# A transformer block on one core: where the first norm of two chunks is scaled and transposed, under a new written-out order

## The chip, the cores and the metric

The kernel runs on one NeuronCore of a Trainium2 chip. The core has a matrix engine (TensorE, called PE; PEld is its weight load), a vector engine (VectorE, DVE), an activation engine (ScalarE, ACT), a general engine (GpSimd, POOL) and an engine that here only issues transfers (SyncE, SP). Each takes its own instructions strictly in order and waits on semaphores for the others. Transfers (DMA) are issued from the queues of SP, ACT or POOL and run beside all engines. The metric is device time in microseconds (us) for one execution. Before the change it is 195.86 us, the median of 3 runs (195.64 to 196.87).

## The reference

The input x has 2048 rows of 512 bf16 numbers. The block is an attention and a gated MLP, each behind a layer norm without weights:

```python
def _layernorm(x, axis=-1, eps=1e-5):
    m = jnp.mean(x, axis=axis, keepdims=True)
    v = jnp.var(x, axis=axis, keepdims=True)
    return (x - m) / jnp.sqrt(v + eps)
...
    h = x + _A_ref(_layernorm(x, axis=-1), A_wqkv, A_wo)
    h2 = h + _B_ref(_layernorm(h, axis=-1), B_W_gate, B_W_up, B_W_down)
```

`_A_ref` is attention with 32 heads of 16, in which a position sees only itself and 7 earlier positions in steps of 2 (`W, dil = 8, 2`), softmax over these 8, then `@ wo`. `_B_ref` is `(relu(x @ W_gate) * (x @ W_up)) @ W_down` with 1376 hidden columns.

## The kernel before

The 2048 rows are worked in four chunks of 512 rows, numbered 0 to 3; a chunk is four row blocks of 128. For each chunk the kernel goes through these stages. The names in brackets are the keys that the code gives its steps, and the prediction uses them with the chunk's number behind a dot.

- First norm: DVE takes the statistics of each row block (`xst`, L467, and `xag`, L470); ACT forms 1/sqrt(variance + eps) by Ln and Exp (`xrl`, L480, `xre`, L484); then x is scaled (`xxn`). The scaling has two forms in `f_xn`: on DVE by a tensor_scalar (L502), or on ACT by an activation with a scale and a bias per row (L499), for which DVE first makes the bias (`xnb`, L488). `LNA[0]` says by chunk which form is taken: before the change, ACT for chunks 1 and 3 and DVE for chunks 0 and 2.
- Transposition of the scaled rows: either PE transposes each row block by four 128x128 matmuls (`xtp`, L531) into a PSUM bank that ACT copies out, two row blocks at a time (`xte`, L547), or a DMA transpose issued by SP does it (`xtd`, L520). `DMAT` names the pairs of row blocks that go by DMA; before, these are both pairs of chunk 3's first norm and five pairs of the second norm.
- q, k and v: 12 groups of four 128x512 matmuls (`qkv0` to `qkv11`, L572), each copied out of its bank by ACT (`qe`, L580).
- Scores: DVE multiplies q by shifted views of k (`pr0`, `pr1`, L635 for chunk 0, L620 else), PE sums over the heads' columns with a selection matrix (`sc0`, `sc1`, L626), ACT takes the exponential (`ex`, L684), PE and ACT form the reciprocal of the softmax sum (`den`, `dl`, `dr`).
- Spreads: 8 DMAs per chunk on SP's queue copy the weights of each head over its 16 columns (`bd0S`, `bd1S`, L744).
- Product with v: DVE multiplies (`mu`, L791 for chunk 0, L776 else); for chunks 0 to 2 an accumulating DMA issued by POOL adds one half of the result to the other (`ta`, L819); DVE adds up the rest (`tree`, L779) and for chunk 0 scales (`om`, L783).
- Output projection on PE (`wo`, L855, L858), residual and row sums (`rs`), second norm (`hnm`, `hsq`, `hxn`, `htp`), and the MLP: gate and up products (`mm`, L928 and L895), ACT copies and Relu, DVE product (`gu`, L956), down product (`dn`, L978), last addition and the stores (`os`).

The late weights, the up and the down matrix, are loaded by four steps on SP's queue (`ldu`, `ldd`). They wait for a step of POOL that reads a result of chunk 0 (`lg`, L837 and L838).

The order of the work is not found while the kernel runs. Each step gets a rank by its number of creation from the table `RANK`, and every engine carries out its own steps in the order of their ranks. A planner places them with assumed durations; its times only decide which of several equal buffers a step gets: 8 PSUM banks are shared by all matmul outputs, 5 large buffers by products and spreads, 5 row buffers by scaled rows.

Of the kernel before, what the change touches and what calls it, by code (L numbers as in the profile page):

```python
# [17 lines left out]
RANK = [  # L18
# [38 lines left out]
]  # L57


# [143 lines left out]
def kernel(  # L203
# [171 lines left out]
    NHALF = 6  # L375
    XT = (3.5, 3.65, 5.6, 6.1, 8.5, 8.9, 9.4, 9.9, 15.9, 17.4)
    WT = (7.55, 7.55, 5.0, 14.2, 18.7, 25.5, 22.0, 29.0)
    DMAT = (('h',2,0),('h',2,2),('h',3,0),('h',3,2),('h',1,0),('x',3,0),('x',3,2))

    EARLY = (1, 2, 3)  # L380

# [12 lines left out]
    TTM, DTG, ATE = 0.0845, 0.35, 0.3  # L394
    LASTC = (D // 2, 3 * D // 4)

    LNA = ((0, 1, 0, 1), (0, 0, 0, 0))


    MM, TP = 0.2165, 0.057  # L400
# [32 lines left out]
    def layernorm(tk, src, dst_slots, pr, groups, on_act, residual=None):  # L433
# [7 lines left out]
        for grp in groups:  # L441
# [72 lines left out]
            for j0 in range(lo, hi, step):  # L514
                if (ln, tk, j0) in DMAT:
                    for j in range(j0, min(j0 + step, hi)):
# [38 lines left out]
    for tk in range(NCK):  # L555
# [3 lines left out]
        groups = XG[tk]  # L559
        xnT, xev = layernorm(tk, xload[tk], xnT_s, lnp, groups, LNA[0][tk])  # L560

# [314 lines left out]

        hnT, hev = layernorm(tk, hd, hnT_s, base + 52, HG[tk], LNA[1][tk], residual=sm)

# [186 lines left out]
```

## Time and profile before

| | before |
|---|---|
| median of 3 runs | 195.86 us (195.64 to 196.87) |
| the profiled execution | 197.74 us |
| its span, first to last instruction | 195.7 us |
| mean granted TensorE clock | 0.998 |
| busy: PE, DVE, ACT, POOL | 187.2, 148.6, 116.7, 18.9 us |
| instructions | 3063 |

The span is what the profile shows of one execution on the core; the execution's own time is 2.0 us longer. This execution was 1.9 us slower than the median of the runs, so a difference that is worked out from its rows is set against 197.74 us and then carried over to the median. In rows of a timeline the first number is the start in us from the span's beginning and the second how long the group of instructions lasted; what stands in brackets is the idle time of the engine before them and what ended it. A row of a group gives busy time, mean ns of one and idle time before. The time in which a matmul counts as busy overlaps that of the next one: back to back, a 128x512 matmul takes the engine forward by 0.216 us, though its own duration reads 379 ns.

### The profile page before, as it was taken

What the parts mean: (1) busy time and instruction counts of PE and PEld (TensorE: products, weight loads), DVE (VectorE), ACT (ScalarE), POOL (GpSimd) and SP (SyncE); (2) the same over time, 40 slices, a digit from 0 to 9 for tenths busy, and PEclk for the clock granted to TensorE, in tenths of its full rate; (3) what the DMA queues carried; (4) which work ended last, traced back from release to release, by engine and by line L of the source; (5) the groups of instructions that cost most, each with busy time, mean ns of one, the idle gap of its engine ahead of it and who ended that gap; (6) DMA issues with size and microseconds to landing.
All of it is one profiled execution on the core that took longest, in us unless ns stands there. A gap on an engine that the chain in (4) does not pass through costs nothing.

```text
span 195.7 us, 3063 instructions
## 1 busy us (share of the span) xinstructions
PE 187.2 (96%) x1113; PEld 97.2 (50%) x1133; DVE 148.6 (76%) x240; ACT 116.7 (60%) x241; POOL 18.9 (10%) x35
## 2 busy tenths in 40 slices
PE   7699998999989999999999999999999999999994
PEld 7686453655344444454444644444544545544543
DVE  6899959999999999998998747999965601422332
ACT  3589896676879675875337668622569701358500
POOL 3000000560000013100034110003000000000000
PEclk9999999999999999999999999999999999999999
DMA  6689565699924426936569977225000430041015
GB/s 200 217 247 369 178 151 115 130 198 206 385 88 93 122 57 126 183 67 151 120 117 183 192 147 174 54 54 93 17 0 0 107 80 30 0 144 44 0 30 161
DMA packets 25214, 24.61 MB, mean 126 GB/s; under 512 B 11408, under 2 KB 21488, under 8 KB 25200
## 3 DMA queue, kind: packets, MB, share of 16 engines
q1 hardware_dynamic: 22176, 16.26, 29.9%
q0 software_dynamic: 2304, 7.34, 20.7%
q10 hardware_dynamic: 720, 0.82, 1.3%
q8 instruction: 9, 0.15, 0.4%
q14 instruction: 5, 0.04, 0.1%
HBM read 8.42 MB, written 2.10 MB: 54 GB/s over the span
## 4 chain that ended last, share of the span: by engine, by line
PE 70%; DVE 12%; DMA 10%; issue 3%; SPq 1%; POOL 1%; ACTq 0%; DVEq 0%; POOLq 0%
PE bank L928 35%; PE bank L978 19%; PE bank L855 6%; DMA big<-big 4%; DVE big L635 4%; DMA x_sm<-in_A_x_dram 4%; PE bank L572 4%; PE bank L895 3%; PE bank L626 3%; DVE big L791 2%; DMA big<-ex 2%; DVE big L620 2%; DVE st L467 1%; SPq L744 1%; PE bank L531 1%
## 5 line engine op out<-in xcount | busy, mean ns | idle before, releaser
L928 PE MATMUL bank<-quad,wgu_sb 128*128 128x512 bf16 x311 | 71.2, 379 | 0.4
L928 PEld LDWEIGHTS <-wgu_sb 128*128 128x128 bf16 x320 | 31.0, 98 | 36.5 <-issue 0.8
L978 PE MATMUL bank<-wd_sb,gT 128*128 128x512 bf16 (+3 forms) x195 | 39.4, 355 | 0.1
L935 ACT ACTIVATE gr<-bank 128x512 bf16<-128x512 f32 x40 | 23.4, 603 | 19.1 <-PE bank L928 17.8
L572 PE MATMUL bank<-quad,wqk_sb 128*128 128x512 bf16 (+1 forms) x150 | 29.2, 345 | 0.6 <-ACT rs L480 0.4
L932 ACT CAST up_sb<-bank 128x512 bf16<-128x512 f32 x40 | 22.7, 590 | 10.7 <-PE bank L928 9.9
L978 PEld LDWEIGHTS <-gT 128*128 128x128 bf16 (+1 forms) x198 | 18.4, 98 | 19.6 <-issue 0.4
L620 DVE TENSOR_TENSOR big<-quad,kT 128x4096 bf16<-128x4096 bf16 x12 | 27.2, 2283 | 0.0
L776 DVE TENSOR_TENSOR big<-big,vT 128x4096 bf16<-128x4096 bf16 x12 | 27.2, 2286 | 0.0
L956 DVE TENSOR_TENSOR gT<-gr,up_sb 128x1024 bf16<-128x1024 bf16 x20 | 13.6, 688 | 14.9 <-ACT gr L935 14.1
L572 PEld LDWEIGHTS <-wqk_sb 128*128 128x128 bf16 x152 | 16.8, 113 | 11.3 <-issue 0.9
L819 POOL DMA_DIRECT2D big<-big x12 | 10.5, 875 | 83.7 <-DVE big L776 53.6
L991 DVE TENSOR_TENSOR row<-x_sm,bank 128x512 bf16<-128x512 bf16 (+2 forms) x10 | 5.6, 580 | 16.3 <-PE bank L978 16.3
L779 DVE TENSOR_TENSOR big<-big 128x1024 bf16<-128x1024 bf16 (+2 forms) x24 | 17.1, 731 | 0.6 <-DMA big<-big 0.4
L572 PE MATMUL bank<-quad,wv_sb 128*128 128x512 bf16 x60 | 15.1, 380 | 0.3 <-issue 0.2
L855 PE MATMUL bank<-wo_sb,quad 128*128 128x512 bf16 x62 | 14.7, 379 | 0.1
L866 DVE SCALAR_TENSOR_TENSOR x_sm<-x_sm,bank 128x512 bf16<-128x512 bf16 x12 | 8.3, 688 | 4.5 <-PE bank L855 4.4
L467 DVE BATCH_NORM_STATS2 st<-x_sm 128x6 f32<-128x512 bf16 x16 | 10.4, 680 | 1.2 <-DMA x_sm<-in_A_x_dram 1.2
L791 DVE TENSOR_TENSOR big<-big,vT 128x2048 bf16<-128x2048 bf16 x8 | 9.5, 1217 | 2.3 <-DMA big<-ex 2.2
L580 ACT CAST kT<-bank 128x512 bf16<-128x512 f32 x16 | 9.3, 595 | 3.1 <-PE bank L572 1.5
L456 ACT ACTIVATE row<-x_sm,mv 128x512 bf16<-128x512 bf16 x12 | 8.6, 720 | 2.8 <-DVE mv L448 2.3
L502 DVE TENSOR_SCALAR row<-x_sm,mv,rs 128x512 bf16<-128x512 bf16 x24 | 9.0, 407 | 1.7 <-ACT rs L484 1.7
(77 smaller groups left out, 166.6 us busy)
## 6 DMA issues: line engine op xcount, KB each, us to landing
big<-big POOLq DMA_DIRECT2D x12, 512.0 KB, 4.8
big<-ex SPq DMA_DIRECT2D x32, 128.0 KB, 2.7
wgu_sb<-in_B_W_gate_dram SPq DMA_DIRECT2D x2, 688.0 KB, 8.3
wgu_sb<-in_B_W_up_dram SPq DMA_DIRECT2D x2, 688.0 KB, 8.7
wd_sb<-in_B_W_down_dram SPq DMA_DIRECT2D x2, 640.0 KB, 9.4
x_sm<-in_A_x_dram SPq DMA_DIRECT2D x2, 512.0 KB, 5.5
x_sm<-up_sb POOLq DMA_DIRECT2D x4, 256.0 KB, 3.7
out_dram<-x_sm SPq DMA_DIRECT2D x4, 256.0 KB, 2.3
```

Source lines behind the costliest of these rows:

```text
L467: V.bn_stats(out=st.t[:], in_=x_sm[:, tk * BPC + j, :])
L572: nc.tensor.matmul(mm.t[:, lo:hi], lhsT=wv_sb[:, dt, t:D:NT] if c == 2 else wqk_sb[:, dt, c * D + t:(c + 1) * D:NT], rhs=xnT.t[:, dt, lo:h ...
L620: V.tensor_tensor(out=pb.t[:].rearrange("p (t w) s -> p t w s", t=2), in0=q4, in1=k4, op=ALU.mult)
L776: V.tensor_tensor(out=mt.t[:], in0=ab.t[:], in1=v8, op=ALU.mult)
L779: V.tensor_tensor(out=mt.t[:, 0:n, :], in0=mt.t[:, 0:n, :], in1=mt.t[:, n:2 * n, :], op=ALU.add)
L791: V.tensor_tensor(out=mt.t[:, 4 * hf:4 * hf + 4, :], in0=ab.t[:, 4 * hf:4 * hf + 4, :], in1=v4, op=ALU.mult)
L855: nc.tensor.matmul(od.t[:], lhsT=OT.t[:, t, j * P:(j + 1) * P], rhs=wo_sb[:, t, :], start=(t == 0), stop=(t == NT - 1 and tk not in RPE))
L928: nc.tensor.matmul(mm.t[:fs, lo:hi], lhsT=wgu_sb[:, dt, g, ft * P: ft * P + fs], rhs=hnT.t[:, dt, lo:hi], start=(dt == 0), stop=(dt == NT ...
L932: nc.scalar.copy(out=ub.t[:fs, i, :], in_=um.t[:fs, :])
L935: nc.scalar.activation(out=gr.t[:fs, i, :], in_=gm.t[:fs, :], func=ACT.Relu)
L956: V.tensor_tensor(out=gt.t[:fs, 0:n, :], in0=gr.t[:fs, 0:n, :], in1=ub.t[:fs, 0:n, :], op=ALU.mult)
L978: nc.tensor.matmul(od.t[:, c0:c1], lhsT=gts[ft].t[:fs, ft % 2, j * P:(j + 1) * P], rhs=wd_sb[:fs, ft, c0:c1], start=(ft == 0), stop=(ft == ...
```

## The change

Chunk 2's first norm is scaled on ACT too, so that chunks 1 to 3 now are. Chunk 3's first norm is transposed by PE and copied out by ACT, no longer by DMA. The rank table is replaced as a whole: it has 751 entries in place of 748, since chunk 2 gets one step more (the bias, `xnb`) and chunk 3 six steps (four `xtp`, two `xte`) in place of four (`xtd`).

```diff
 RANK = [
     0, 1, 2, 3, 4, 5, 6, 7, 8, 9, 10, 11, 12, 13, 14, 15, 16, 17, 18, 19,
     20, 22, 23, 25, 29, 30, 32, 21, 24, 26, 28, 31, 35, 38, 40, 27, 33, 36, 37, 42,
-    47, 51, 34, 39, 41, 43, 46, 50, 55, 45, 52, 87, 90, 75, 82, 83, 88, 56, 57, 60,
-    65, 44, 48, 59, 62, 74, 78, 85, 94, 53, 80, 89, 95, 63, 72, 70, 76, 110, 126, 97,
+    47, 51, 34, 39, 41, 43, 46, 49, 54, 45, 58, 87, 90, 82, 85, 89, 94, 52, 56, 60,
+    63, 44, 48, 61, 66, 57, 76, 83, 88, 53, 75, 79, 84, 64, 73, 71, 77, 109, 120, 93,
...
-    DMAT = (('h',2,0),('h',2,2),('h',3,0),('h',3,2),('h',1,0),('x',3,0),('x',3,2))
+    DMAT = (('h',2,0),('h',2,2),('h',3,0),('h',3,2),('h',1,0))
...
-    LNA = ((0, 1, 0, 1), (0, 0, 0, 0))
+    LNA = ((0, 1, 1, 1), (0, 0, 0, 0))
```

Sorted by rank, the two tables give each engine its order. The stretches that differ in ways the prediction uses are these (a dash joins a stage and its row block or part where that matters; "x4" stands for all four):

```
DVE before: mk0.0, xag.3, xst.2 x2, xnb.3, xst.2, mu2c.0, xag.2 x2, mu3c.0, xst.2, xag.2 x2, mu1a.0, mu3a.0,
            xxn.2 x2, mu1c.0, xxn.2 x2, mu2a.0, mu0a.0, mu0c.0, tree3.0 x2, pr0.1, om3.0, tree1.0, pr0.1, tree2.0,
            ..., om0.0, pr1.1 x2
DVE after:  mk0.0, xag.3 x4, xst.2 x2, xnb.3, xst.2 x2, xag.2 x2, mu3c.0, mu2c.0, mu3a.0, xag.2 x2, mu1c.0, mu1a.0,
            xnb.2, mu0c.0, mu2a.0, mu0a.0, pr0.1, tree3.0 x2, om3.0, tree1.0 x2, om1.0, pr0.1, tree2.0, pr1.1,
            tree2.0, tree0.0, om2.0, tree0.0, om0.0, pr1.1
ACT before: xrl.3, xre.3, qe, xxn.3 x4, qe x3, xrl.2, qe, xre.2, qe x3, dl.0, qe x2, xte.2, qe, xte.2, qe, dr.0, qe ...
ACT after:  xrl.3, qe, xre.3, dl.0, xxn.3 x4, dr.0, xte.3 x2, qe, xrl.2, qe, xre.2, qe x2, xxn.2, qe x3, xxn.2, qe,
            xxn.2, qe, xxn.2, qe, xte.2 x2, qe ...
PE before:  ..., sc0.0, qkv of chunks 1 and 3 with xtp.2 x2 twice between, qkv of chunks 2 and 3, sc0.1, wo x3, sc1.1, wo0.0, qkv ...
PE after:   ..., den.0, qkv x4 of chunk 1, xtp.3 x4, qkv of chunks 1 and 3 with xtp.2 between, sc0.1, qkv x4, wo2.0,
            wo3.0, sc1.1, wo0.0, qkv, den.1, wo1.0, qkv x4, sc1.2, qkv, htp.0 x4, qkv x2, sc0.2, mm ...
POOL before: ta3.0, ta1.0, ta2.0, ta0.0, lg, ta3.1 ...      POOL after: ta3.0, ta1.0, ta2.0, lg, ta0.0, ta0.1 ...
SP before:  spreads of chunk 0, xtd.3 x4, ldu, ldd, ldu, ldd, spreads of chunk 1, spreads of chunk 2 ...
SP after:   spreads of chunk 0, ldu, ldu, ldd, spreads of chunk 1, ldd, spreads of chunk 2 ...
```

68 rows, old and new, of the table RANK are left out of this document.

## The prediction

> **What bounds the kernel now.** I read the busy shares, then PE in order of time, then DVE, ACT and POOL at the places where PE stands still. From the page, the shares and the rows in 40 slices of 4.9 us:
>
> ```profile
> PE 187.2 (96%) x1113; PEld 97.2 (50%) x1133; DVE 148.6 (76%) x240; ACT 116.7 (60%) x241; POOL 18.9 (10%) x35
> ...
> PE   7699998999989999999999999999999999999994
> ...
> DVE  6899959999999999998998747999965601422332
> ACT  3589896676879675875337668622569701358500
> ```
>
> PE is full from the end of the eleventh slice (54 us) to the last. That it is full of work and not of waiting shows in the chain of waits, where 128x512 matmuls follow each other by 0.216 us (8 in 1.73 us). So the end moves by what PE gets to do, plus the time in which it stands still, and by little else. Where it stands still after its start, in PE's order of time:
>
> ```profile
> 31.22 2.13 PE L572 MATMUL bank<-quad,wqk_sb 128*128 128x512 bf16 x8
> 34.25 0.72 PE L531 MATMUL bank<-identity,row 128*128 128x128 bf16 x8 [0.89 <-DVE row L502]
> ...
> 53.19 0.38 PE L858 MATMUL bank<-x_sm,identity 128*128 128x512 bf16 x1
> 54.56 1.05 PE L626 MATMUL bank<-big,sel 128*32 128x512 bf16 x16 [0.99 <-DVE big L620]
> ```
>
> The 8 matmuls at 31.22 need 8 x 0.216 = 1.73 us, so PE is done at 32.95 and starts again at 34.25: 1.30 us lost, of which the row shows 0.89. It waits for the scaled rows of chunk 2, which DVE makes (L502). Then 0.99 us are lost at 53.57, for the products of chunk 1's second half of scores. In windows of 10 us PE's idle time between 20 and 70 is 0.17, 1.03, 0.05, 1.04 and 0.11 us, 2.40 in all. From 70 to 190 nothing but breaks of 0.05 us is left.
>
> DVE makes the rows late because they stand behind products:
>
> ```profile
> 28.17 1.23 DVE L791 TENSOR_TENSOR big<-big,vT 128x2048 bf16<-128x2048 bf16 x1 [2.24 <-DMA big<-ex]
> ...
> 33.78 0.73 DVE L502 TENSOR_SCALAR row<-x_sm,mv,rs 128x512 bf16<-128x512 bf16 x2
> 34.43 1.22 DVE L791 TENSOR_TENSOR big<-big,vT 128x2048 bf16<-128x2048 bf16 x1
> 35.56 0.73 DVE L502 TENSOR_SCALAR row<-x_sm,mv,rs 128x512 bf16<-128x512 bf16 x2
> ```
>
> **The change, part by part.** (1) *Chunk 3's transposes come to PE.* 16 more L531 matmuls. In the chain, 16 of them take 0.89 us (at 63.28). PE is the bound, nothing covers them: **+0.89**. The two copies out (L547) go to ACT, part 3.
>
> (2) *Four scalings leave DVE.* Two L502 take DVE forward by 0.65 us in the chain, four by 1.30; `xnb` adds about 0.08 (0.15 alone, mostly overlapped). DVE's list also takes one statistic and four `xag` from between the products to before them. That is 0.62 + 0.2 us that now lies in DVE's wait of 2.24 us for the first spread (28.17): before that wait one more L467 (0.62) and two L470 (0.1 each) are to be done from 25.9 on, ending near 27. So `mu0` ends near 37.5 instead of 39.7. For PE it means that chunk 2's rows come from ACT, and the 1.30 us should go, if ACT is in time: **-1.30**.
>
> (3) *ACT gets the work.* Four L499 in a row took 2.93 us (25.35 to 28.28), two L547 1.93 us (63.77 to 65.70): 4.86 us more, all between 29 and 42. Between 20 and 50 ACT was idle for 1.22, 3.04 and 3.42 us, 7.68 in all, so it fits on balance. In order it goes so: `xre.3` near 25.6, `dl.0`, four L499 to 29.3, `dr.0`, two L547 to 31.8. Then copies at 0.49 us each, with `xrl.2` and `xre.2` (0.2 each) done by 33.2. `xnb.2` stands in DVE's list behind six products and comes at 34.0; ACT reaches the first scaling of chunk 2 at 34.1, the last at 39.5, and ends its two L547 at 42. PE meanwhile has its eight banks: I count 22 outputs put in against the copies that empty them, in both orders, and PE would wait some 0.1 us at four or five of them (from 38.9 to 42.0). Behind a waiting scaling on ACT stand copies, and behind those PE, so this is where a loss would come: **+0.4**, between 0 (ACT's former idle time takes all) and 4.86 (none of it).
>
> [...]
>
> (4) *DMA transposes leave SP.* They ran from 28.01 to 33.27, 5.26 us of SP's queue. The next thing in that queue is a weight load at 43.05, which waits for POOL. Nobody waits for the queue: 0. DMA engines stood idle at 34 to 36, so no transfer was held up either: 0, and at the most 0.4 of gain or loss, the one wait of DVE for an accumulation.
>
> (5) *The gate of the late weights (`lg`) now stands before `ta0.0` in POOL's queue.*
>
> ```profile
> 39.99 0.86 POOL L819 DMA_DIRECT2D big<-big  x1 [1.41 <-DVE big L791]
> 40.68 2.29 DVE L620 TENSOR_TENSOR big<-quad,kT 128x4096 bf16<-128x4096 bf16 x1
> 40.83 2.20 POOL L837 COPY wgu_sb<-big 1x4 bf16<-1x4 bf16 x1
> 42.95 0.43 POOL L838 COPY wd_sb<-big 1x11 bf16<-1x11 bf16 x1
> ```
>
> `lg` waits for `tree3.0`: 37.5 + 2.20 (`pr0.1`) + 0.94 = 40.65. L837 lasted 2.20 us and ended when DVE's L620 did; now DVE's next instructions are short (L783 0.42, L779 0.69), so I take `lg` done at 41.75, `ta0.0` issued by 42.6. An accumulation took 4.5 to 8.5 us to land; the 8.5 is `ta0.0` itself, behind three others that kept the DMA engines full from 36 on. Now the three start earlier: landed near 47 to 48.5. DVE comes to `tree0.0` at 47.6 and would end `om0.0` at 49.2, PE comes to `wo2.0` at 49.8: cost 0, up to 1.5 if it lands late. [...] Of the loads, `ldd` goes behind chunk 1's spreads, and is issued by 65; the first down product stands near 84 on PE: 0.
>
> (6) *The stall at 53.57.* `sc1.1` waits for the second `pr1.1`. By sums of row durations, DVE has 1.22 us less before it and PE 0.20 less, and DVE's waits shrink by another 1 us or so (0.44 at `tree0.0`, 0.14 among the products, the 0.8 of part 2 that is already counted). So DVE would be there at 52.0, and PE, without its 1.30, at 52.1: **-0.99**.
>
> (7) *The rest of the order, from 66 us on.* I added up DVE's work ahead of each hand-over and PE's work up to the same place, in both orders, for `wo`, `htp`, the first `mm` of chunks 1 to 3 and the fourth chunk's scores. PE's is 0.66 to 1.54 longer at all of them, DVE's 0.92 to 4.02 shorter, save the denominator of chunk 2, where both grow (by 4.99 and 4.38). The narrowest in the trace of before: chunk 1's `tree` ends at 88.2, `wo` starts at 88.6; both come some 2 us earlier now and the gap stays. No stall is added: 0, up to 1.5 (one miss of the size of those of today) as the other end.
>
> Sum: +0.89 - 1.30 - 0.99 + 0.4 = **-1.0**. Against the profiled execution: 197.74 - 1.0 = 196.7. The median of the runs lies 1.88 lower than that execution: 195.86 - 1.0 = **194.9 us**.
>
> **Rivals.**
>
> *Less than that goes.* Stalls move rather than vanish: the chain through the first output projection, the second norm and `htp.0` was just in time for PE, and it gets one step later by `wo1.0` standing behind `den.1`. For it: in the trace the copy of `htp` waits 0.57 at 63.77. Against it: five groups of fillers follow `wo1.0`. If both stalls come back at another place, the transposes alone are left: +0.89, 196.75 us.
>
> *ACT becomes the bound (the other side).* Between 25 and 50 us its list holds 23.5 us of work in my count, from `xrl.3` to the last copy before `rs2.0`, where it held 19.7, and I leave it no idle time. If hand-overs cost it what they cost before, nothing of its former idle time is usable: +4.86, less the 2.29 of stalls that end beneath it, with the transposes beneath it too: +2.57, 198.4 us. It decides from the point where ACT's delay exceeds 2.29, that is where under 2.57 of the 7.68 us idle can be used. Against it: the idle time of before was mostly waiting for PE and DVE, which are ahead now.
>
> *A late hand-over.* `ta0.0` behind the gate lands 1.5 late, or one of the gaps of part 7 closes: +0.5 to +1.5, some 196.4 to 197.4, and with two of them over 197.8.
>
> *More goes.* All 2.40 idle between 20 and 70 and the 0.4 never lost: 0.89 - 2.40 = -1.5, 194.35; to pass 1% some 0.5 us more would have to be hidden in the stretched rows, such as the 0.41 found at 31.22.
>
> *It doesn't do what it says.* Chunk 2's scaling on ACT is tied to DVE by `xnb.2` behind six products that wait for spreads; if the spreads land later than 28.17, ACT and all copies behind it stand. That would show as ACT idle at 34 and is part of the second case's chance.
>
> **How the numbers follow.** A measurement of this kernel tells a change from none at about 1%, 1.96 us: faster means under 193.9, slower over 197.8. Chances: forecast (194.0 to 195.8) 0.44; less goes (195.8 to 197.2) 0.20; ACT bound (197.2 to 199.5) 0.14, of it 0.12 over 197.8; late hand-over 0.12, half of it over 197.8; more goes (193.2 to 194.3) 0.10, of it 0.07 under 193.9. Faster 0.07, slower 0.12 + 0.06 = 0.18, the same 0.75. The range reaches from 193.9 up to 198.3, which leaves out 0.07 below and some 0.12 above.
>
> **What would show it.** Right: L531 with 88 matmuls and L547 with 9 of two blocks; L499 with 12, L502 with 20; no idle time before L531 near 34; the last `mu` of chunk 0 ending near 37.5; `sc1.1` without its 0.99; the last matmul near 191.9 instead of 192.87. Wrong: PE idle before L572 between 30 and 46 with ACT busy throughout (the second rival), PE idle at the first `wo` with DVE waiting for DMA before L779 (the third), or PE idle anywhere beyond 70. The forecast fails if PE, with 0.89 us more to do, stands still as long as before.

## The result and the profile after

The changed kernel takes **203.43 us** (median of 6 runs, 202.81 to 204.61). The kernel before takes 196.36 us (median of 6 runs, 195.64 to 196.87). The ratio is **1.036, 95% interval 1.033 to 1.039**: 7 us slower, where a gain of 1 us was predicted. The profiled execution took 204.61 us, its span 202.8 us; that of before had 197.74 and 195.7.

First the page of the changed kernel: the busy shares, then the rows of the span in 40 slices, here of 5.07 us.

```profile
PE 191.5 (94%) x1149; PEld 99.1 (49%) x1149; DVE 148.2 (73%) x237; ACT 120.5 (59%) x247; POOL 17.0 (8%) x35
...
PE   8699999999298999999999999999999999999992
...
DVE  6699979997449999998999568699976610225232
...
PEclk9999999999969999999999999999999999999999
```

PE has one hole, in the eleventh slice (51 to 56 us), then a slice with a low clock, and is full from the fourteenth to the end. DVE's two slices of 4 are the eleventh and the twelfth. So the loss sits in one place, and nothing beyond 66 us stalls PE. Next PE in order of time, over the stretch in which PE stood still before the change and over the hole:

```profile
32.94 4.48 PE L572 MATMUL bank<-quad,wqk_sb 128*128 128x512 bf16 x20
...
46.77 1.05 PE L626 MATMUL bank<-big,sel 128*32 128x512 bf16 x16 [0.42 <-ACT kT L580]
47.75 3.64 PE L572 MATMUL bank<-quad,wqk_sb 128*128 128x512 bf16 x16
55.23 1.20 PE L855 MATMUL bank<-wo_sb,quad 128*128 128x512 bf16 x4 [3.83 <-DVE quad L783]
...
56.65 1.91 PE L855 MATMUL bank<-wo_sb,quad 128*128 128x512 bf16 x4
58.92 1.25 PE L626 MATMUL bank<-big,sel 128*32 128x512 bf16 x16
...
62.80 0.38 PE L701 MATMUL bank<-row,same 128*128 128x512 bf16 x1 [0.57 <-DVE row L716]
```

The two stalls of before are gone: 20 matmuls run through from 32.94, over the place where PE had waited 1.30 us for chunk 2's rows, and the scores at 58.92 (`sc1.1`) wait for nothing. In their place PE waits 0.42 us at 46.77 for one of ACT's copies of k, and then 3.83 us ahead of the first output projection (`wo2.0`), for the scaled attention output of chunk 0. Then it runs slowly: four L855 take 1.91 us at 56.65, where they take 1.03 at full clock. The granted clock was 0.50 from 56 to 59 us and 0.81 in the next microsecond. Then 0.57 us more are lost at the denominators of chunk 1 (`den.1`).

The chain that ended last says what the 3.83 us are. Its columns are start, duration and what held the chain:

```profile
42.93 10.40 DMA big<-big
53.32 0.02 issue
53.35 0.69 DVE big L779
54.04 0.34 DVE quad L783
```

It is one transfer: `ta0.0`, the last of chunk 0's four accumulations. Issued at 42.93, landed at 53.33, 10.40 us later. The first three took 4.7, 5.1 and 5.8 us. Before the change the same transfer was issued at 39.99 and took 8.47. POOL shows why it went out so late, and SP what went out just ahead of it:

```profile
37.57 0.86 POOL L819 DMA_DIRECT2D big<-big  x1 [1.21 <-DVE big L791]
41.93 0.45 POOL L837 COPY wgu_sb<-big 1x4 bf16<-1x4 bf16 x1 [3.50 <-DVE big L779]
42.32 0.70 POOL L838 COPY wd_sb<-big 1x11 bf16<-1x11 bf16 x1
42.93 0.55 POOL L819 DMA_DIRECT2D big<-big  x1
```

```profile
42.41 0.88 SPq L310 DMA_DIRECT2D wgu_sb<-in_B_W_up_dram  x2
43.40 0.41 SPq L304 DMA_DIRECT2D wd_sb<-in_B_W_down_dram  x1
```

POOL is free from 38.4 on, and DVE's last product of chunk 0 ends at 38.4, so `ta0.0` could go; but the gate (L837, L838) stands ahead of it in POOL's order and waits 3.50 us for DVE's `tree3.0`. When the gate is through, it lets go of two loads of 688 KB and one of 640 KB, 2.06 MB in all, and the accumulation of 512 KB starts beside them.

DVE, meanwhile, and ACT behind it:

```profile
48.97 0.42 DVE L779 TENSOR_TENSOR big<-big 128x512 bf16<-128x512 bf16 x1
53.35 0.69 DVE L779 TENSOR_TENSOR big<-big 128x1024 bf16<-128x1024 bf16 x1 [3.96 <-DMA big<-big]
...
59.64 0.15 DVE L448 TENSOR_SCALAR mv<-sm 128x1 f32<-128x1 f32 x1 [2.27 <-ACT x_sm L864]
```

```profile
57.46 0.58 ACT L580 CAST kT<-bank 128x512 bf16<-128x512 f32 x1 [6.98 <-DVE big L620]
```

DVE reaches `tree0.0` at 49.39 and stands for 3.96 us. All its other work of this stretch is queued behind, among it the second-half product of chunk 1 (`pr1.1`, L620, 55.09 to 57.37). And ACT stands for 6.98 us in front of a copy of chunk 2's k (`qe5.2`): by the code the copy writes one row of `kT`, and `pr1.1` reads that row and the next in one access that spans the columns of chunk 2 as well, so the copy waits until the product is done (the wait is in the row; that this access is the reason was not tried by itself). The residual and row sums of chunk 0 (`rs2.0`, L864) are queued behind that copy, and the second norm's start on DVE (L448) waits 2.27 us for them.

Measured from the first 128x256 matmul to the end of the last matmul, PE's stretch is 184.67 us before and 190.22 after: +5.55 of the 7.1 us of span. The rest lies outside it: the first of these matmuls starts 0.83 us later (it waits for row blocks of x; over the profiles of this study it varies from 7.9 to 10.1 us, in both orders), and from the last matmul to the end of the span it is 3.56 us in place of 2.83.

### The profile page after: what moved, and what is told of

It is laid out like the page before. It is cut to its first block, busy times and chain, and to the rows that moved or that the text cites. A ratio compares the mean times of both kernels' runs of the same rounds, so it can differ in the third digit from the quotient of the medians.

```text
span 202.8 us, 3111 instructions
## 1 busy us (share of the span) xinstructions
PE 191.5 (94%) x1149; PEld 99.1 (49%) x1149; DVE 148.2 (73%) x237; ACT 120.5 (59%) x247; POOL 17.0 (8%) x35
## 4 chain that ended last, share of the span: by engine, by line
PE 67%; DMA 5%; DVE 3%; ACT 1%; issue 0%; ACTq 0%
PE bank L928 34%; PE bank L978 19%; PE bank L855 6%; DMA big<-big 5%; PE bank L572 3%; PE bank L895 3%; DVE big L620 2%; PE bank L626 2%; PE bank L531 1%; ACT quad L580 1%; DVE big L779 1%; PE bank L701 0%; DVE quad L783 0%; ACT kT L580 0%; DVE row L716 0%
## 5 line engine op out<-in xcount | busy, mean ns | idle before, releaser
L928 PE MATMUL bank<-quad,wgu_sb 128*128 128x512 bf16 x320 | 72.2, 379 | 0.0
L572 PE MATMUL bank<-quad,wqk_sb 128*128 128x512 bf16 (+1 forms) x152 | 29.9, 345 | 0.4 <-ACT rs L480 0.4
L620 DVE TENSOR_TENSOR big<-quad,kT 128x4096 bf16<-128x4096 bf16 x12 | 27.3, 2285 | 0.5 <-ACT kT L580 0.3
L779 DVE TENSOR_TENSOR big<-big 128x1024 bf16<-128x1024 bf16 (+2 forms) x24 | 17.0, 730 | 4.1 <-DMA big<-big 4.0
L855 PE MATMUL bank<-wo_sb,quad 128*128 128x512 bf16 x64 | 16.0, 398 | 3.8 <-DVE quad L783 3.8
L572 PE MATMUL bank<-quad,wv_sb 128*128 128x512 bf16 x64 | 16.0, 380 | 0.0
L580 ACT CAST kT<-bank 128x512 bf16<-128x512 f32 x16 | 9.3, 592 | 8.9 <-DVE big L620 8.7
L855 PEld LDWEIGHTS <-quad 128*128 128x128 bf16 x64 | 6.3, 101 | 12.9 <-DVE quad L783 4.3
L547 ACT COPY quad<-bank 128x1024 bf16<-128x1024 bf16 (+1 forms) x12 | 10.5, 916 | 1.7 <-PE bank L531 1.6
```

Of the source, the lines that this page charges most:

```text
L547: nc.scalar.copy(out=o, in_=i)
L572: nc.tensor.matmul(mm.t[:, lo:hi], lhsT=wv_sb[:, dt, t:D:NT] if c == 2 else wqk_sb[:, dt, c * D + t:(c + 1) * D:NT], rhs=xnT.t[:, dt, lo:h ...
L580: nc.scalar.copy(out=o, in_=mm.t[:])
L620: V.tensor_tensor(out=pb.t[:].rearrange("p (t w) s -> p t w s", t=2), in0=q4, in1=k4, op=ALU.mult)
L779: V.tensor_tensor(out=mt.t[:, 0:n, :], in0=mt.t[:, 0:n, :], in1=mt.t[:, n:2 * n, :], op=ALU.add)
L855: nc.tensor.matmul(od.t[:], lhsT=OT.t[:, t, j * P:(j + 1) * P], rhs=wo_sb[:, t, :], start=(t == 0), stop=(t == NT - 1 and tk not in RPE))
```

## The experiments

The theory after the result: **G**, the gate ahead of `ta0.0` costs most of it, and **K**, the copy of k ahead of `rs2.0` costs the rest. Rivals: the work that was added or moved is itself too much; the half clock is the price; the order is worse further on. In the diffs an index of `RANK` names a step; the comment says which.

**1. The accumulation ahead of the gate.**

```diff
+RANK[128], RANK[106] = RANK[106], RANK[128]  # lg, ta0 of chunk 0
```

> The kernel after, with one exchange in POOL's order: the last accumulation of chunk 0 (ta0.0) stands before the gate of the late weights (lg), as in the kernel before. Theory G (the gate sends 2.06 MB of weights onto the DMA engines just ahead of ta0.0, which then lands 10.4 us after its issue): ta0.0 is issued near 38.5 and lands before 47.6, DVE's wait of 3.96 us before L779 falls under 0.5, PE's 3.83 us before L855 fall under 0.5, the granted clock stays at 1.0 between 50 and 60, and the time falls by 5 to 6.5 us to 197 to 198.5. Rival Q (the fourth accumulation lands late because it is the fourth in a row on full DMA engines, 8.5 us in the kernel before): it still lands after 50 and the time stays within 1 us of 203.4. Rival A (ACT's added work is the cost, the stall only shows where the delay comes out): the stall moves to another place, time above 201.

Measured: 200.74 us, ratio 1.015 (1.009 to 1.021). `ta0.0` was issued at 37.64 and landed at most 8.2 us later, and neither DVE nor PE waits for it. That is some 2% of the time, the larger part of the loss, but not all. What is left shows on PE and ACT (the added line moves the line numbers by one):

```profile
57.43 0.38 PE L702 MATMUL bank<-row,same 128*128 128x512 bf16 x1 [2.16 <-DVE row L717]
57.65 1.86 PE L856 MATMUL bank<-wo_sb,quad 128*128 128x512 bf16 x4
```

```profile
52.10 0.58 ACT L581 CAST kT<-bank 128x512 bf16<-128x512 f32 x1 [2.92 <-DVE big L621]
```

With the first wait gone, the second comes forward: the copy of k still stands ahead of the row sums, and now PE pays 2.16 us for it at `den.1`, where it paid 0.57. Behind it the clock falls, against the expectation: it was granted at 0.50 from 58 to 61 us, and four L856 take 1.86 us.

**2. Late, but without company.** The gate's two copies stay where they are and write to a scratch tile, so `ta0.0` goes out as late as in the changed kernel; the loads are let go by a second pair of copies that reads a later result.

```diff
-                nc.gpsimd.tensor_copy(out=wgu_sb[0:1, :, 1, 0:1], in_=mt.t[0:1, 0:1, 0:NT].rearrange("p a s -> p s a"))
+                nc.gpsimd.tensor_copy(out=scr[0:1, 0:NT, 0:1], in_=mt.t[0:1, 0:1, 0:NT].rearrange("p a s -> p s a"))
...
+            late = (f_lg2, [oev[0]], [mts[0]])
...
+    lg2 = add(("lg2", 0), "POOL", 0.3, late[0], late[1], 0, use=late[2], lat=0.1)
+    for n in LATE:
+        for o in wload[n]:
+            o.deps.append(lg2)
```

> The kernel after, with POOL's two small copies left where they are (they now write into a scratch tile), so that ta0.0 is issued as late as in the kernel after, near 42.9; the late weights wait for a second pair of copies that reads the last result of chunk 0, near 49. Theory G, in the form that the loads on the DMA engines are what delays ta0.0: it lands 4.5 to 5.5 us after its issue, near 48, DVE's wait is under 1 us, time 197 to 199. Its other form, that the late issue alone costs it (one place in POOL's queue): it lands after 50, time above 201. The up weights are needed near 66 and would land near 57, so nothing new should wait for them.

Measured: 200.87 us, ratio 1.017 (1.011 to 1.023).

```profile
42.44 0.55 POOL L823 DMA_DIRECT2D big<-big  x1
```

Its landing, from the list of transfers issued between 42 and 54 us (the last number is us to landing), then DVE's rows and PE's wait:

```profile
big<-big POOLq DMA_DIRECT2D x1, 512.0 KB, 4.2
```

```profile
48.48 1.02 DVE L783 TENSOR_TENSOR big<-big 128x512 bf16<-128x512 bf16 x2
```

```profile
58.26 0.38 PE L703 MATMUL bank<-row,same 128*128 128x512 bf16 x1 [2.17 <-DVE row L718]
```

PE waits 2.17 us at `den.1`, as in run 1, and the times of the two runs are alike. The same transfer, issued at 42.44, landed in **4.2 us** (46.6), before DVE came for it at 48.9, and DVE's rows run on without a wait. So it is not the late issue alone that hurts: it is being late *and* beside 2.06 MB of loads. Alone the 512 KB took 4.2 us, beside the loads 10.40; how the loads make it longer no run shows.

**3. The half clock.** Sixteen matmuls without use ahead of the first output projection, so that PE is busy during the wait.

```diff
+                if tk == 0 and j == 2:
+                    for _ in range(16):
+                        nc.tensor.matmul(od.t[:], lhsT=warm[:], rhs=wo_sb[:, 0, :], start=True, stop=True)
```

> The kernel after, with 16 matmuls of 128x512 that compute nothing needed, placed on PE in front of the first output projection, into the bank that it then overwrites: 16 x 0.216 = 3.45 us of the 3.83 us in which PE stood still. The stall itself stays. Theory C (after the stall the clock was granted at half, 0.50 from 56 to 59, and 3.14 us of matmuls took 4.88 us): the granted clock stays at 1.0, the rows of L855 show 379 ns again, and the time falls by 1.2 to 2.0 us against the kernel after. Rival (the slow rows come from something else, such as weights loaded late): no change within 0.5 us.

Measured: 205.68 us, ratio 1.042 (1.036 to 1.047). The expected gain did not come.

```profile
54.02 1.04 PE L858 MATMUL bank<-wo_sb,quad 128*128 128x512 bf16 x4 [0.33 <-DVE quad L783]
...
61.59 0.45 PE L701 MATMUL bank<-row,same 128*128 128x512 bf16 x1 [2.21 <-DVE row L716]
61.84 1.91 PE L858 MATMUL bank<-wo_sb,quad 128*128 128x512 bf16 x4
...
73.68 2.55 PE L931 MATMUL bank<-quad,wgu_sb 128*128 128x512 bf16 x11
```

The first output projection ran at full clock, but `den.1` came no earlier: from `wo2.0` to `den.1` it is 7.57 us in both kernels, here with a wait of 2.21 us, in the changed kernel with slow matmuls and a wait of 0.57. Where PE waited for DVE and ACT anyway, the slow matmuls cost nothing. The clock fell at `den.1` instead (0.50 from 62 to 65 us), and there it has a price. From `den.1` to the first gate product (L931) PE takes 12.09 us, in the changed kernel 10.40 (62.80 to 73.20): 1.69 us more, about what its stretch is longer by (191.79 against 190.22). Run 1, where the clock also falls at `den.1`, takes 12.09 for the same work, and run 2, where it stays at 1.00, 10.40. The times agree: of the eight executions of runs 1 and 2, the three with a mean granted clock of 0.999 or 1.000 took 199.90 to 200.45 us, the five others, at 0.988 to 0.990, 200.70 and more. So in the changed kernel the half clock is a mark of the wait and costs nothing of its own, and in run 1 it is 1.69 us of what is left.

**4. The same exchange the other way round, in the kernel before.** There the accumulation stands first; now the gate does.

```diff
+RANK[128], RANK[106] = RANK[106], RANK[128]  # lg, ta0 of chunk 0
```

> The kernel before, with the same exchange the other way: lg before ta0.0 on POOL. Theory G: ta0.0 is issued near 43.4 in place of 39.99, behind the loads, lands after 51 in place of 48.46, DVE waits 2 to 6 us before L779 in place of 0.44, and the time rises by 2 to 7 us. Rivals Q and A: within 1 us of the kernel before.

Measured: 201.32 us, ratio 1.018 (1.012 to 1.024). The gate's first copy takes 2.20 us, `ta0.0` goes out at 43.82 and lands 7.9 us later. DVE's and PE's waits for it:

```profile
DVE big L780 <- DMA big<-big: 3.2, 1, 3.2
```

```profile
53.44 1.06 PE L856 MATMUL bank<-wo_sb,quad 128*128 128x512 bf16 x4 [2.71 <-DVE quad L784]
```

The same mechanism, without any other part of the change: an exchange of two neighbours in POOL's list costs some 3.5 us (1.8% of 196). PE's stretch is 188.21 us, 3.54 longer than before: 2.71 are the wait, and most of the rest comes behind it, where the clock fell to 0.50 for some 3 us.

**5. The copy of k moved as well.** Run 1 and, on ACT, `qe5.2` behind the last of chunk 0's row sums.

```diff
+RANK[128], RANK[106] = RANK[106], RANK[128]  # lg, ta0 of chunk 0
+RANK[433] = 262.5  # qe5.2 behind rs3.0
```

> As the run with the accumulation first, and one step more: ACT's copy of chunk 2's k, third part (qe5.2), goes behind the second row sum (rs3.0) on ACT; in the run with the accumulation first it stood ahead of rs2.0 and waited 2.92 us for DVE's product pr1.1, which reads the k buffer of chunk 1. Theory K (that wait holds back rs2.0, DVE then stands 2.27 us in front of hnm.0 and everything behind it, and PE 2.16 us in front of den.1, after which the clock is granted at about half): all three waits fall under 0.5 us, the granted clock stays at 1.0, and the time falls by 2.5 to 3.6 us, to 0.996 to 1.004 of the kernel before. Rival (the copy is only the last of several things that are late there): the wait before den.1 stays above 1 us, ratio above 1.008.

Measured: 196.95 us, ratio **1.003 (1.000 to 1.006)**. PE at the places of the waits (lines moved by two):

```profile
51.09 1.03 PE L857 MATMUL bank<-wo_sb,quad 128*128 128x512 bf16 x4
...
53.34 1.05 PE L628 MATMUL bank<-big,sel 128*32 128x512 bf16 x16
...
56.27 0.38 PE L703 MATMUL bank<-row,same 128*128 128x512 bf16 x1
```

No brackets: `wo2.0`, `sc1.1` and `den.1` all start without a wait. PE's stretch is 183.42 us. That is 4.14 shorter than in run 1 (187.56): 2.16 of wait, 1.69 of slow matmuls and 0.29 of smaller things. One exchange of two ranks and one step moved account for the whole loss. The stretch is also 1.25 shorter than in the profile of before, but the times do not show it: by them the new order does not win either.

**6. The copy of k alone**, with the gate left ahead of `ta0.0`.

```diff
+RANK[433] = 262.5  # qe5.2 behind rs3.0
```

> The changed kernel with the copy of k behind rs3.0 alone; the gate stays ahead of the accumulation. Theory A (the two losses lie on one chain of DVE, one behind the other, and the gate's is first): PE still waits 3.8 us for the first output projection; the wait of 2.27 us of DVE at the second statistics of chunk 0 goes, and of PE's waits only the 0.57 at the denominators; the time is 0.6 us lower than that of the changed kernel, some 202.8, ratio to before 1.030 to 1.036. Theory B (each costs by itself what it cost in the step from the run with the accumulation first to the run with both): 2.5 to 3.5 us lower, some 200.4, ratio 1.018 to 1.024.

Measured: 203.08 us, ratio 1.032 (1.026 to 1.037), as theory A has it. PE's waits:

```profile
PE bank L856 <- DVE quad L784: 3.3, 1, 3.3
```

The wait at `den.1` is gone and DVE's 2.27 us too, and by the times that is worth little while `ta0.0` is late. In the profiled execution the clock stayed at 1.00 and PE's stretch is 188.47 us, 1.75 shorter than in the changed kernel; the other three executions had a mean granted clock of 0.991 or 0.992, and no time of the four shows such a gain clearly (203.06; 201.74 to 203.35). With runs 1 and 5 this makes a table of four, ratios to before:

| | k copy ahead of the row sums | behind them |
|---|---|---|
| gate ahead of `ta0.0` | 1.036 (the change) | 1.032 |
| `ta0.0` ahead of the gate | 1.015 | 1.003 |

The two waits lie on one chain. By differences the exchange is worth 2.1% alone and 2.9% with the other remedy in place, the move 0.4% and 1.2%; the 0.4% lies within the intervals (1.033 to 1.039 and 1.026 to 1.037).

**7. The stores.** In run 5 the span ends 3.37 us after the last matmul, before 2.83. Two stores of finished blocks go ahead of an earlier one.

```diff
+RANK[400] = 734.4  # os3.1 ahead of os2.3
+RANK[392] = 734.7  # os1.1 ahead of os2.3
```

> As the run with the k copy later, and two stores of chunk 1 (os3.1, os1.1, 256 KB each) go ahead of os2.3 in SP's queue, as they or their like stood in the kernel before. Theory S (between the last matmul's end and the end of the span lie 2.84 us in the kernel before and 3.4 to 3.6 in all kernels with the new order, because two stores of 256 KB are issued in the last 7 us): that stretch falls to 2.8 to 3.0, and the time by 0.4 to 0.8 us against the run with the k copy later. Rival: the last small store sets the end alone, no change within 0.3 us.

Measured: 196.6 us, ratio 1.000 (0.997 to 1.003). The end after the last matmul was 3.5 us, no shorter (in a profiled execution of 199.94 us), and the difference to run 5 lies within the intervals. Where the 0.5 us at the end come from stays open.

**8. Chunk 2's scaling on ACT, alone, in the order of before.**

```diff
-    LNA = ((0, 1, 0, 1), (0, 0, 0, 0))
+    LNA = ((0, 1, 1, 1), (0, 0, 0, 0))
...
+RANK.insert(411, 172.5)  # xnb.2, in front of the place of the first xxn.2
```

> The kernel before with chunk 2's first norm scaled on ACT, in the old order (the new bias step stands where DVE's first scaling stood), the transposes of chunk 3 still by DMA. By the prediction's parts 2 and 3: DVE has 1.2 us less, PE loses less than 0.5 of the 1.30 us at 34, time lower by 0.5 to 1.5 us. Rival D (the four accumulations keep the DMA engines full from 36 on and set when DVE gets to tree0.0; the rows still come from ACT no earlier in this order): DVE's gain turns into waiting for the accumulation, 1 us or more in place of 0.44, and the time stays within 0.6 us.

Measured: 197.79 us, ratio 1.007 (1.004 to 1.010).

```profile
34.30 0.40 PE L532 MATMUL bank<-identity,row 128*128 128x128 bf16 x4 [0.43 <-ACT row L500]
35.49 0.40 PE L532 MATMUL bank<-identity,row 128*128 128x128 bf16 x4 [0.79 <-ACT row L500]
```

PE waits for the rows as before, only from ACT: 1.22 us. And DVE, which has less to do, waits 1.3 us for accumulations. `sc1.1`, though, starts without a wait (at 55.05), and PE's stretch is 184.39 us, 0.28 shorter. The time is 0.7% longer all the same, and the profile does not show why. Without a new order the move brings nothing.

**9. Chunk 3's transposes on PE, alone, in the order of before.**

```diff
-    DMAT = (('h',2,0),('h',2,2),('h',3,0),('h',3,2),('h',1,0),('x',3,0),('x',3,2))
+    DMAT = (('h',2,0),('h',2,2),('h',3,0),('h',3,2),('h',1,0))
...
+RANK[582:590] = [153, 161, 142, 146, 161.5, 148, 154, 145, 169, 169.5]  # chunk 3: xtp at the ranks of the xtd, xte behind
```

> The kernel before with chunk 3's first norm transposed by PE and copied out by ACT, in the old order (the transposes at the ranks of the DMA transposes), chunk 2 still scaled on DVE. By the prediction's part 1: PE has 0.89 us more and nothing covers it, time higher by 0.5 to 1.2 us. Rival: the 16 matmuls and two copies fall into time in which PE would wait anyway, within 0.3 us; or ACT's two copies delay others, over 1.5 us.

Measured: 199.0 us, ratio 1.012 (1.008 to 1.017).

```profile
31.45 1.02 PE L573 MATMUL bank<-quad,wqk_sb 128*128 128x512 bf16 x4 [1.10 <-ACT quad L548]
```

PE has the 16 transposes to do and waits 1.10 us for their copies on ACT. Its stretch is 185.40 us, 0.73 longer than before, but the time rose by some 2.4 us, which is what the expectation's second rival (ACT's copies delay others) has. In runs 5, 8 and 9 alike the ratio gives 1.6 to 1.8 us more than the stretch. A stretch is that of one execution, and the profiled one of before took 197.74 us, 1.3 above the median of its runs here (196.46); whether that is the reason stays open.

**10. Run 5 with chunk 3's transposes back on DMA.** If PE is full, leaving out its 0.89 us of transposes should win.

```diff
-    DMAT = (('h',2,0),('h',2,2),('h',3,0),('h',3,2),('h',1,0))
+    DMAT = (('h',2,0),('h',2,2),('h',3,0),('h',3,2),('h',1,0),('x',3,0),('x',3,2))
...
+RANK[583:593] = [146, 158, 153, 159, 149, 157, 155, 161]  # chunk 3: xtd at the ranks of the xtp, no xte
```

> The new order with the accumulation ahead of the gate and the copy of k behind rs3.0, and chunk 3's x transposed by DMA again (two on each side of the former places, no L531 of chunk 3, no L547 of it). Theory A (PE is full in this order, so that its work sets the end): 16 transposes of 0.89 us leave PE, 1.93 us leave ACT, and the stretch from the first 128x256 matmul to the last one is 182.5 us (183.42 with the transposes on PE); the time is 0.5 to 0.9 us lower than with them, some 196.0, ratio to before 0.996 to 1.000. Theory B (the DMA transposes come too late or get in the way of the accumulations of chunk 0): PE waits for the first projection of chunk 3 or DVE for an accumulation, the stretch is 183.4 us or longer, ratio 1.002 or more.

Measured: 203.63 us, ratio 1.032 (1.026 to 1.038): theory B, and by far more than it had. PE, then SP and POOL (lines moved by three):

```profile
31.29 1.03 PE L575 MATMUL bank<-quad,wv_sb 128*128 128x512 bf16 x4
38.11 6.98 PE L575 MATMUL bank<-quad,wqk_sb 128*128 128x512 bf16 x20 [5.80 <-DMA quad<-row]
```

```profile
28.48 5.26 SPq L523 DMA_TRANSPOSE quad<-row  x4
```

```profile
32.33 1.01 POOL L822 DMA_DIRECT2D big<-big  x1 [20.12 <-DVE mv L473]
34.69 0.86 POOL L822 DMA_DIRECT2D big<-big  x1 [1.35 <-DVE nb L491]
```

The new order takes chunk 3's first projections at 32 us, right after the rows are scaled. The four DMA transposes occupy SP to 33.7; the last was issued at 32.53, at the moment when the first accumulation went out, and landed 5.45 us later (2.4 to 2.6 us for all of them before the change). PE stood for 5.80 us and then ran 20 matmuls in 6.98 us where they take 4.48 at full clock, a price of 2.5 us for the clock (0.50 from 37 to 43 us). PE's stretch is 190.66 us, 7.2 longer than in run 5. So the transposes on PE are what the new order stands on: their 0.89 us buy rows in time.

No kernel that was run beats the one before.

## Why the prediction was wrong

By its own steps:

- **(5), the gate: the step that failed.** "Landed near 47 to 48.5 ... cost 0, up to 1.5". The issue was nearly right (42.93 for "by 42.6"), the landing was not: 53.33. The step took the 8.5 us of before as the result of the three accumulations ahead, and so expected less once these were through. It priced the loads only by when they end (`ldd`, needed at 84) and not by what they do to a transfer beside them. The row for it was on view: SP's load at 43.05 and `ta0.0` in flight from 39.99 to 48.46. Run 2 shows the loads as the cause (4.2 against 10.40 us), runs 1 and 4 the size: 2.1% and 1.8%. The rival *late hand-over* had this place and this kind of loss, with a price of 0.5 to 1.5 us, where the exchange was worth 3.5 to 4 us, some of it by the clock, which no term had. The prediction's own sign for it, PE idle at the first `wo` with DVE waiting for DMA before L779, is what the profile shows.
- **(3), ACT, and (7), the hand-overs further on.** ACT was weighed as a sum of work against idle time, and its waits were looked for between 34 and 42 us, where PE's rows show gaps of about 0.1 us at most: there the term of +0.4 was nearer to 0. PE waits 0.42 us for ACT at 46.77, for a copy of k that had itself waited 1.76 us for DVE (L620); that the sizes agree is luck. What was not looked at is a wait of ACT for DVE: `qe5.2` ahead of `rs2.0`. The trace of before had this kind of wait, 1.5 us of `kT` L580 behind DVE's L620 in two places; there no row shows PE waiting for it. Runs 5 and 6 against 1 and the changed kernel show 0.4% (within the intervals) to 1.2%.
- **(1), +0.89.** Run 9's stretch is 0.73 longer, its time some 2.4 us; the stretch fits the term, the time does not, and the difference stays open. What the sum did not say is that the term could not be taken back alone in this order (run 10).
- **(2), -1.30, and (6), -0.99: held.** Both stalls are gone in the changed kernel and in run 5. The products of chunk 0 end at 38.4, and at 37.5 in the prediction, of which 0.83 is the later start. Run 8 shows that (2) comes from the new order together with the move, not from the move; (6) shows with the move alone.
- **(4), 0.** SP's queue held up nobody, as said.
- **(7) beyond 66 us: held** in the row of slices. The breaks of 0.05 us that the prediction saw there need not be lost time: the profile of before has 1113 matmuls for 1133 weight loads, and a missing record would leave a gap of 2 x 0.216 - 0.379 = 0.05 us; the changed kernel's (1149 and 1149) shows no such breaks. The end behind the last matmul, 0.5 to 0.7 us longer, was not foreseen.

Terms (1), (2), (3) and (6) together gave -1.0; run 5, which has them without the two new waits, has a stretch of PE 1.25 us shorter. Its time is equal to that of before all the same (1.003). In the two profiles the later start (9.31 against 8.19) and the end (+0.54) take the gain away; but the start varies from execution to execution, so for the times themselves this explains nothing. So the two stalls went as forecast, and in one execution's stretch the size fits; that they are worth 1.0 us of the time no run shows. The loss came from what the order put in front of one transfer and one sum.

## What to carry to other kernels

When a step that releases large loads changes places with a transfer that somebody waits for, price the transfer beside the loads, and not by its time alone: look in the trace for the time it took with and without company. For each instruction that an order moves forward on an in-order engine, ask what it waits for and who is queued behind it; adding up busy time against idle time does not show such a wait. And before a slower clock is blamed, look whether the engine would only have been early for its next wait: some 3 us at half clock cost nothing ahead of a wait (the changed kernel) and 1.7 us where none followed (runs 1 and 3).

## What had not been expected of the hardware

- The 512 KB accumulation landed in 4.2 us alone (run 2), in 8.47 behind three others, with loads beside it from 43.05 on (before), and in 10.40 beside 2.06 MB of loads that had been issued from 0.5 us ahead of it.
- A DMA transpose that landed in 2.4 to 2.6 us in the kernel before took 5.45 us beside an accumulation that started in the same half microsecond (run 10). That the accumulation is the cause was not tried by itself.
- The length of PE's pause does not say whether the clock falls. After 2.16 us (run 1), 2.21 us (run 3) and 2.71 us (run 4) it was granted at 0.50 for some 3 us; after 2.17 us (run 2) and 3.32 us (run 6) it stayed at 1.00. What decides it these runs do not show.
